# Turning normalised rows by DMA instead of by TensorE in a fused attention and gated-FFN kernel

## The chip, the cores and the metric

The kernel runs on one core of a Trainium2 chip, as one launch. The metric is device time in microseconds (us) of that core. The program has five instruction streams that run side by side and meet at semaphores: TensorE (PE, with its weight loads listed apart as PEld), VectorE (DVE), ScalarE (ACT), GpSimd (POOL) and SyncE (SP), which here only issues DMAs.

## The reference, cut to what matters

One transformer block over 2048 tokens of 512 channels, with 32 heads of 16 channels and a feed-forward width of 1792, all inputs in bf16:

```python
def _layernorm(x, axis=-1, eps=1e-5):
    m = jnp.mean(x, axis=axis, keepdims=True)
    v = jnp.var(x, axis=axis, keepdims=True)
    return (x - m) / jnp.sqrt(v + eps)
...
    def _A_ref(x, wqkv, wo):
        ...
        qkv = (lambda x, *d: x.transpose(*d))((x @ wqkv).reshape(B, S, 3, H, Dh), 2, 0, 3, 1, 4)
        q, k, v = qkv[0], qkv[1], qkv[2]
        scores = jnp.einsum("bhqd,bhkd->bhqk", q, k) * (Dh ** -0.5)
        p = _softmax(scores, axis=-1)
        o = jnp.einsum("bhqk,bhkd->bhqd", p, v)
        return (lambda x, *d: x.transpose(*d))(o, 0, 2, 1, 3).reshape(B, S, D) @ wo

    def _B_ref(x, w_gate, w_up, w_down):
        g = jnp.einsum("bsd,df->bsf", x, w_gate)
        u = jnp.einsum("bsd,df->bsf", x, w_up)
        h = _sigmoid(g) * u
        return jnp.einsum("bsf,fd->bsd", h, w_down)

    x = A_x
    h = x + _A_ref(_layernorm(x, axis=-1), A_wqkv, A_wo)
    h2 = h + _B_ref(_layernorm(h, axis=-1), B_w_gate, B_w_up, B_w_down)
    return h2
```

Both layer norms work on rows (a token on a partition, its 512 channels along the free axis). The projections behind them contract over channels, so the normalised rows have to be turned: channels on partitions, tokens along the free axis. Those turns are what this case is about.

## The kernel before, in words

**Tiling.** Tokens are cut into 16 row tiles of 128, and into four chunks (`c` = 0 to 3) of 512 for the first layer norm. The turned first layer norm of chunk `c` is the tile `xnT[c]`. Attention takes 2048 "units" of 128 keys by 512 queries for a head (or the same area as two key tiles by 256 queries). For each unit PE makes scores into PSUM, ACT (line 1466) or DVE makes them exponentials, and PE multiplies those by the values (line 1260). ACT takes two or three units in one instruction, 128x1024 or 128x1536. DVE takes one unit at a time (line 1284, into a tile `J`), and POOL (line 1305), sometimes with another DVE add (line 1329), derives from `J` further terms of the same exponential. PE then multiplies two or three terms of such a unit instead of one.

**The first layer norm.** Chunk 0 is done in a prologue. For chunks 1 to 3 DVE takes the statistics, POOL makes the reciprocal root and the normalised rows (`pool_apply`, line 589, tile `xn0`), PE turns two row tiles with eight 128x128 transposes (line 732), and DVE copies them from PSUM to `xnT[c]` (line 735). Then PE makes the keys of the first head group (`early_k`, line 745) and the values (`prep_v`, line 318) of that chunk. Attention is already running on the chunks that are there.

**The second layer norm and the FFN.** The FFN runs in eight parts of 256 tokens. For parts 0 to 6 `wo_ln` makes the output projection, adds the residual, normalises on DVE (line 824, tile `hn`), turns each of the two row tiles with four transposes on PE (line 307), and copies them on DVE to half of `xnT[0]` (line 832, read through `hn_of`). `ffn_up` then reads them as the moving operand of the gate and up matmuls (line 841) and `ffn_down` makes the output (line 859). Part 7 comes after the last attention unit, in a tail written out by hand, with turns of its own on PE.

**The order.** The order of every engine is fixed when the program is built. A planner in the kernel keeps a clock for each engine (`T`), charges a cost for each step, and interleaves: for each ACT instruction ("tile n" below) it writes the next scores, then fills PE with value products and with background steps (turns, projections, FFN), each once its inputs are due. It also decides which units go to DVE. The dictionary `PLAN` overrides some of its choices, by tile number and step. What it writes is final: an engine whose next instruction isn't ready waits, whatever stands behind. SP has one queue for the loads of the gate and up weights (`wgu`, line 849), the residual rows (`xr`, line 785), the output stores (line 867) and the rest, in the order in which the planner wrote them.

The planner knows a step that ends later than its job by a fixed time:

```python
    class Later:
        def __init__(self, job, ns):
            self.job, self.ns = job, ns

        @property
        def end(self):
            return None if self.job.end is None else self.job.end + self.ns
```

Of the kernel before, what the change touches and what calls it, by code (L numbers as in the profile page):

```python
# [22 lines left out]
PLAN = {124: 2, 159: 2, 178: 9, 193: 3, 194: 3, 207: 2, 224: 9, 239: 2, 334: 1, 354: 1, 384: 9, 385: 9, 416: 3, 464: 9, 466: 1, 476: 1, 512: 3, 527: 2, 529: 9, 530: 3, 540: 1, 559: 1, 641: 5, 720: 2, 737: 3, 769: 4, 800: 3, 801: 4, 833: 5, 865: 9, 942: 2, 945: 9, 1041: 3, 1056: 3, 1071: 2, 1105: 9, 1169: 9, 1345: 4, 1409: 4, 1519: 2, 1520: 4, 1567: 2, 1580: 1, 1598: 3, 1616: 2, 1618: 9, 1632: 3, 1633: 4, 1808: 4, 1824: 1, 1855: 2, 1857: 1, 1888: 9, 1889: 2, 1921: 4, 1922: 3, 1936: 3, 1952: 5, 1968: 4, 2176: 9, 2208: 5, 2224: 9, 2240: 1, 2258: 5, 2284: 2, 2304: 3, 2336: 9, 2352: 2, 2368: 4, 2400: 9, 2401: 3, 2402: 2, 2416: 3, 2432: 1, 2449: 4, 2588: 2, 2604: 2, 2640: 4, 2658: 4, 2688: 9, 2722: 1, 2736: 4, 2780: 1, 2786: 1, 2799: 2, 2831: 2, 2833: 1, 2865: 1, 2866: 5, 2928: 3, 2959: 2, 2976: 4, 2992: 2, 3025: 3, 3056: 3, 3058: 4, 3072: 1, 3102: 3, 3121: 3, 3152: 3, 3164: 1, 3185: 9, 3198: 3, 3200: 4, 3246: 1, 3248: 4, 3249: 2, 3260: 1, 3280: 4, 3297: 4, 3308: 1, 3505: 9, 3551: 2, 3567: 2, 3596: 1, 3649: 3, 3664: 1, 3680: 4, 3695: 1, 3714: 3, 3777: 3, 3808: 2, 3824: 2, 4017: 2, 4046: 3, 4112: 3, 4113: 2, 4145: 3, 4208: 4, 4220: 1, 4224: 3, 4240: 4, 4241: 1, 4284: 1, 4334: 2, 4384: 1, 4526: 3, 4588: 1, 4593: 4, 4608: 5, 4652: 1, 4671: 2, 4719: 2, 4720: 1, 4764: 1, 4768: 4, 4796: 1, 4815: 2, 4816: 1, 4848: 1, 4892: 1, 4912: 5, 4992: 3, 5008: 3, 5009: 3, 5072: 3, 5089: 4, 5090: 4, 5201: 1, 5233: 1, 5263: 1, 5292: 1, 5343: 2, 5356: 1, 5406: 1, 5422: 3, 5425: 4, 5455: 2, 5521: 1, 5548: 1, 5553: 4, 5617: 4, 5628: 1, 5649: 1, 5713: 3, 5728: 3, 5792: 5, 5809: 2, 5824: 1, 5858: 9, 5890: 9, 5918: 2, 6002: 4, 6017: 4, 6047: 2, 6048: 2, 6064: 2, 6140: 1, 6156: 2, 6160: 2, 6208: 4, 6304: 4, 6321: 1, 6383: 1, 6431: 2, 6433: 4, 6524: 1, 6529: 9, 6544: 4, 6545: 4, 6608: 2, 6673: 1, 6684: 1, 6720: 4, 6796: 2, 6800: 3, 6848: 3, 6865: 1, 6896: 5, 6927: 2, 6956: 1, 6960: 4, 6978: 5, 7106: 2, 7120: 3, 7122: 4, 7164: 1, 7200: 4, 7248: 9, 7406: 1, 7440: 4, 7454: 3, 7490: 9, 7553: 3, 7585: 4, 7598: 3, 7648: 4, 7649: 4, 7660: 1, 7663: 1, 7696: 4, 7712: 4, 7729: 4, 7759: 1, 7760: 3, 7762: 2, 7776: 3, 7777: 1, 7809: 2, 7824: 1, 7826: 9, 7841: 9, 7857: 9, 7873: 9, 7921: 3, 7969: 1, 7985: 4, 8000: 4, 8065: 4, 8076: 1, 8128: 4, 8144: 1, 8156: 2, 8161: 9, 8176: 2, 8192: 1, 8193: 2, 8204: 2, 8240: 2, 8272: 4, 8274: 4, 8287: 1, 8289: 4, 8304: 1, 8332: 2, 8400: 4, 8512: 2, 8578: 9, 8620: 2, 8623: 2, 8652: 2, 8656: 1, 8703: 2, 8766: 1, 8768: 2, 8800: 1, 8844: 1, 8849: 3, 8863: 2, 8879: 2, 8880: 3, 8914: 2, 8926: 1, 8930: 3, 8944: 3, 8976: 4, 8992: 3, 8994: 9, 9008: 1, 9025: 1, 9040: 4, 9042: 5, 9074: 2, 9120: 4, 9152: 1, 9168: 3, 9201: 4, 9232: 3, 9308: 1, 9312: 4, 9346: 1, 9425: 5, 9438: 2, 9488: 1, 9500: 1, 9520: 4, 9521: 3, 9538: 9, 9564: 1, 9569: 9, 9598: 1, 9612: 1, 9726: 2, 9740: 1, 9760: 4, 9777: 4, 9826: 4, 9872: 3, 9888: 3, 9904: 4, 9916: 1, 9969: 3, 9983: 2, 10064: 3, 10108: 2, 10114: 9, 10144: 4, 10176: 3, 10192: 3, 10193: 1, 10239: 2, 10242: 3, 10268: 2, 10272: 2, 10273: 3, 10321: 9, 10384: 2, 10386: 4, 10428: 1, 10498: 1, 10510: 1, 10512: 4, 10513: 1, 10524: 2, 10542: 1, 10544: 2, 10560: 3, 10561: 9, 10591: 2, 10640: 5, 10673: 1, 10753: 3, 10784: 3, 10785: 3, 10849: 1, 10864: 4, 10944: 1}  # L23
# [121 lines left out]
def kernel(  # L145
# [11 lines left out]
    nc = tc.nc  # L157
# [51 lines left out]
    xnT = [const.tile([P, DC, QC], BF16, name=f"xnT{c}") for c in range(NQC)]  # L209
    KT = [const.tile([P, S], BF16, name=f"KT{p}") for p in range(NP)]  # L210
# [100 lines left out]
    def proj8(ps, w_sb, p, c, a=0, b=DC):  # L311
        for d in range(a, b):
            nc.tensor.matmul(ps, lhsT=w_sb[:, d, p * P:(p + 1) * P], rhs=xnT[c][:, d, :],  # L313
                             start=(d == 0), stop=(d == DC - 1))

    def v_mm(ps, t, a=0, b=DC):
        for d in range(a, b):
            nc.tensor.matmul(ps, lhsT=xnT[t // TQ][:, d, (t % TQ) * P:(t % TQ + 1) * P],  # L318
                             rhs=wv_sb[:, d, :], start=(d == 0), stop=(d == DC - 1))
# [73 lines left out]
    def copy0(c, i, eng):  # L393
        eng(out=xnT[c][:, :, i * P:(i + 1) * P], in_=buf["t", c, i])
        free0(("t", i))

    def proj0(which, i):
        ps = buf[which] if which in buf else buf.setdefault(which, bank0(which))
        for d in range(DC):
            E.matmul(ps[:, i * P:(i + 1) * P], lhsT=w0[:, which, d, :], rhs=xnT[0][:, d, i * P:(i + 1) * P],  # L400
                     start=(d == 0), stop=(d == DC - 1))
# [185 lines left out]
    def pool_apply(c, i):  # L587
        xn = buf["xn", c, i] = prep.tile([P, D], BF16, name="xn0", bufs=4)
        nc.gpsimd.tensor_scalar(out=xn[:], in0=xb[c][:, i, :], scalar1=mvs[c][:, i, 0:1],
                                scalar2=rstds[c][:, i:i + 1], op0=ALU.add, op1=ALU.mult)  # L590

    TINY = 400.0
# [62 lines left out]
    DRAIN = 170.0  # L655
    OVER = 300.0
# [50 lines left out]
    def early_ln(c):  # L707
# [14 lines left out]

        done["ap", c] = ja

        def turn():
            for i in range(0, TQ, 2):
                yield pe(4, pm_new, ja[i], ja[i + 1], ns=8 * 75.0)
                ps = pm_tile()
                pt = ps.bitcast(BF16).rearrange("p (i b q) -> p i b q", i=2, b=DC)
                for k in range(2):  # L730
                    for b in range(DC):
                        nc.tensor.transpose(out=pt[:, k, b, :],
                                            in_=buf["xn", c, i + k][:, b * P:(b + 1) * P],
                                            identity=ident_bf[:])
                pm_out(dve(605, lambda i=i, pt=pt: nc.vector.tensor_copy(
                    out=xnT[c][:, :, i * P:(i + 2) * P].rearrange("p b (i q) -> p i b q", i=2),
                    in_=pt), st["mark"]))
                done["x", c, i // 2] = [st["pms"][-1]]
        return turn()

    def early_k(c):
        yield pe(4, pm_new, After(("x", c, 0)), After(("x", c, 1)))
        ps = pm_tile()
        for d in range(DC):
            nc.tensor.matmul(ps, lhsT=w0[:, 0, d, :], rhs=xnT[c][:, d, :],
                             start=(d == 0), stop=(d == DC - 1))
        done["k0", c] = [pm_out(dve(603, lambda: nc.vector.tensor_copy(
            out=KT[0][:, c * QC:(c + 1) * QC], in_=ps), st["mark"]))]
# [39 lines left out]
    def hn_of(r):  # L788
        o = r % 2 * PW
        return xnT[0][:, :, o:o + PARTS[r][2]]  # L790

    def wo_ln(r):
# [27 lines left out]
        hns, jh = {}, {}  # L820

        def apply(i):
            hn = hns[i] = fwork.tile([P, D], BF16, name="hn", bufs=2)
            nc.vector.tensor_scalar(out=hn[:], in0=h[:, i, :], scalar1=mv[:, i, 0:1],
                                    scalar2=rstd[:, i:i + 1], op0=ALU.subtract, op1=ALU.mult)
        for i in range(n):
            jh[i] = dve(455, lambda i=i: apply(i), jr[i])
        jx = []
        for i in range(n):
            yield pe(2, pm_new, jh[i], ns=300.0)  # L830
            pt = transpose4(pm_tile(), hns[i])
            jx.append(pm_out(dve(335, lambda pt=pt, i=i: nc.vector.tensor_copy(
                out=hn_of(r)[:, :, i * P:(i + 1) * P], in_=pt), st["mark"])))
        done["hn", r] = jx
# [4 lines left out]
    def gate_mm(ps, w, r, a=0, b=DC):  # L839
        for d in range(a, b):  # L840
            nc.tensor.matmul(ps[:, 0:PARTS[r][2]], lhsT=w[:, d, :], rhs=hn_of(r)[:, d, :],  # L841
# [153 lines left out]
    def place_now(job):  # L995
# [6 lines left out]
        elif isinstance(job, Job) and job.end is None:  # L1002
            for d in job.deps:
                place_now(d)
            if job.end is None and job.ready() is not None:
# [35 lines left out]
    PART = 12 + 8 * FC // 2 + 14 * (PW // P)  # L1041
# [86 lines left out]
    def finish_group(qc, g):  # L1128
# [13 lines left out]
        def turn():  # L1142
# [13 lines left out]
            if g == NG - 1 and qc < NCH - 1:  # L1156
                rs = [r for r in range(NR) if PARTS[r][0] == qc]
                for k, r in enumerate(rs):
                    queue(wo_ln(r), ("wo", r), 6 * (PARTS[r][2] // P), k)
# [249 lines left out]
    for c in range(1, NQC):  # L1409
        queue(lns[c], ("ln", c), 8)  # L1410
# [210 lines left out]
    for i in range(n):  # L1621
        pt = transpose4(gu[i], hnl[i])
        dst = hn_of(r)[:, :, i * P:(i + 1) * P]
# [76 lines left out]
```

## Time and profile before

| what | value |
|---|---|
| time, median of 3 runs | 742.64 us (742.5 to 743.09) |
| the profiled execution: its time | 743.0 us |
| its span in the trace | 741.1 us |
| PE busy | 707.3 us |
| DVE busy | 672.1 us |
| ACT busy | 708.0 us |
| POOL busy | 418.1 us |
| granted TensorE clock | full in all 40 slices |
| share of DMA queue q1 | 18.3% of 16 engines |

"Busy" is the union of an engine's instructions in the trace. Matmuls overlap and their ends are modelled, so PE's share says little of how near its peak it is. A group's row gives the count, the busy time of the group and the mean duration of one. Where instructions of one engine overlap, busy divided by count is less than the mean. The time is about 1.9 us more than the span of the same execution, which begins and ends with the core's own instructions.

### The profile page before, as it was taken

Reading aid. Unit: us, or ns where it says so; the run is one execution under the profiler, and the core shown is the slowest. Engines: PE = TensorE matmul, PEld = TensorE weight load, DVE = VectorE, ACT = ScalarE, POOL = GpSimd, SP = SyncE. Lnnn points to the kernel's source line nnn. Section 1 sums busy time; section 2 is a strip of 40 time slices with the busy share of each in tenths; the row PEclk is TensorE's granted clock in tenths of the full one; section 3 lists DMA queues with packets and bytes.
Section 4 is the critical chain, followed back from the end, with each engine's and each line's share of the span. In section 5 each row is a group of like instructions: output and inputs, shape, how many; then the busy total and the mean of one; then the engine's idle time right before and its main releaser. Section 6 shows DMA issues by size and latency. Waiting matters only on the chain.

```text
span 741.1 us, 26337 instructions
## 1 busy us (share of the span) xinstructions
PE 707.3 (95%) x11142; PEld 342.0 (46%) x11213; DVE 672.1 (91%) x1334; ACT 708.0 (96%) x789; POOL 418.1 (56%) x711
## 2 busy tenths in 40 slices
PE   8989998888999999999999999999999999999997
PEld 3332223443555445544555455444554455455555
DVE  6988999999999999998999899989999999999952
ACT  7989999999999999999999999999999999999962
POOL 2533466677466557655655556556655666756710
PEclk9999999999999999999999999999999999999999
DMA  7000005000123103310222123201231034003270
GB/s 241 1 1 2 1 1 172 4 2 2 31 79 88 31 10 101 88 31 15 73 59 60 38 65 103 59 9 36 76 88 31 17 101 116 24 10 88 59 214 18
DMA packets 68923, 41.59 MB, mean 56 GB/s; under 512 B 3520, under 2 KB 68800, under 8 KB 68800
## 3 DMA queue, kind: packets, MB, share of 16 engines
q1 hardware_dynamic: 68512, 39.59, 18.3%
q8 instruction: 89, 1.46, 0.8%
q14 instruction: 34, 0.28, 0.1%
q10 hardware_dynamic: 288, 0.26, 0.1%
HBM read 37.75 MB, written 2.10 MB: 54 GB/s over the span
## 4 chain that ended last, share of the span: by engine, by line
PE 56%; ACT 26%; DVE 13%; issue 3%; POOL 1%; ACTq 0%; POOLq 0%; DVEq 0%
ACT pt L1466 19%; PE PS L1102 19%; PE PS L1260 15%; PE PS L841 10%; DVE J L1284 6%; PE PS L859 5%; ACT xnT L1466 3%; PE PS L313 2%; PE PS L318 2%; DVE J L1329 1%; ACT QTb L1466 1%; PE PS L780 1%; ACT th L871 1%; POOL J L1305 1%; PE PS L474 1%
## 5 line engine op out<-in xcount | busy, mean ns | idle before, releaser
L1305 POOL INT64_ADD J<-J x642 | 400.0, 636 | 267.2 <-DVE J L1284 228.3
L1466 ACT ACTIVATE pt<-PS 128x1024 f16<-128x1024 f32 (+2 forms) x517 | 517.4, 1137 | 5.5 <-PE PS L1102 4.8
L1284 DVE TENSOR_SCALAR J<-PS 128x512 int16<-128x512 f32 x613 | 403.0, 677 | 19.6 <-PE PS L1102 15.0
L1102 PE MATMUL PS<-QT,KT 32*128 32x256 bf16 (+1 forms) x3712 | 265.3, 276 | 17.0 <-ACT pt L1466 9.7
L1260 PE MATMUL PS<-J,Vaug 128*17 128x256 f16 (+1 forms) x3128 | 221.0, 279 | 1.6 <-DVE xs L1168 0.6
L1260 PE MATMUL PS<-pt,Vaug 128*17 128x256 f16 (+1 forms) x2048 | 189.8, 278 | 0.5 <-issue 0.5
L1102 PEld LDWEIGHTS <-KT 32*128 32x128 bf16 x3840 | 91.5, 92 | 202.6 <-issue 197.2
L1260 PEld LDWEIGHTS <-Vaug 128*17 128x17 bf16 x5797 | 129.8, 90 | 78.8 <-issue 70.7
L841 PE MATMUL PS<-xnT,wgu 128*128 128x256 bf16 x784 | 113.4, 274 | 0.6 <-DVE qd L768 0.2
L1466 ACT ACTIVATE xnT<-PS 128x1024 f16<-128x1024 f32 (+1 forms) x88 | 96.5, 1140 | 0.1
L1329 DVE TENSOR_TENSOR J<-J 128x1024 f16<-128x1024 f16 (+1 forms) x107 | 77.7, 727 | 9.1 <-POOL J L1305 8.5
L841 PEld LDWEIGHTS <-wgu 128*128 128x128 bf16 x784 | 64.0, 97 | 39.8 <-issue 34.2
L859 PE MATMUL PS<-wd,hT 128*128 128x512 bf16 x173 | 51.6, 383 | 2.2 <-issue 2.1
L1260 PE MATMUL PS<-xnT,Vaug 128*17 128x256 f16 x358 | 53.1, 273 | 0.0
L871 ACT ACTIVATE th<-PS 128x512 f32<-128x512 f32 (+1 forms) x63 | 39.2, 622 | 8.8 <-DVE hT L854 5.6
L1466 ACT ACTIVATE QTb<-PS 128x1024 f16<-128x1024 f32 x39 | 42.9, 1100 | 0.1
L913 DVE SCALAR_TENSOR_TENSOR hT<-th,PS 128x512 bf16<-128x512 f32 x49 | 33.1, 675 | 1.7 <-PE PS L841 1.6
L1168 DVE STREAM_TRANSPOSE xs<-PS 128x256 f32<-128x256 f32 (+1 forms) x60 | 27.3, 455 | 2.3 <-PE PS L1260 2.0
L1466 ACT ACTIVATE xb<-PS 128x1024 f16<-128x1024 f32 (+2 forms) x26 | 26.8, 1098 | 1.4 <-PE PS L1102 0.9
L1466 ACT ACTIVATE pe<-PS 128x1024 f16<-128x1024 f32 (+2 forms) x26 | 25.5, 1027 | 2.5 <-PE PS L1102 1.9
L1260 PE MATMUL PS<-QTb,Vaug 128*17 128x256 f16 x156 | 25.8, 274 | 0.0
L1139 DVE TENSOR_TENSOR o<-xs,rsum 128x128 bf16<-128x128 f32 (+1 forms) x60 | 22.7, 378 | 2.1
(129 smaller groups left out, 416.4 us busy)
## 6 DMA issues: line engine op xcount, KB each, us to landing
wgu<-in_B_w_gate_dram SPq DMA_DIRECT2D x49, 256.0 KB, 3.0
wgu<-in_B_w_up_dram SPq DMA_DIRECT2D x49, 256.0 KB, 3.5
out_dram<-ob SPq DMA_DIRECT2D x16, 128.0 KB, 2.0
wd<-in_B_w_down_dram SPq DMA_DIRECT2D x1, 1792.0 KB, 7.6
xr<-in_A_x_dram SPq DMA_DIRECT2D x14, 128.0 KB, 3.6
xb<-in_A_x_dram SPq DMA_DIRECT2D x6, 256.0 KB, 6.5
J<-in_B_w_gate_dram SPq DMA_DIRECT2D x4, 384.0 KB, 6.0
J<-in_B_w_up_dram SPq DMA_DIRECT2D x4, 384.0 KB, 6.8
```

The lines of the kernel that those rows point to most:

```text
L841: nc.tensor.matmul(ps[:, 0:PARTS[r][2]], lhsT=w[:, d, :], rhs=hn_of(r)[:, d, :], start=(d == 0), stop=(d == DC - 1))
L859: nc.tensor.matmul(ps, lhsT=hT[:, f, i * P:(i + 1) * P], rhs=wd[:, f, :], start=(f == 0), stop=(f == FC - 1))
L871: nc.scalar.activation(out=th[:, 0:ps.shape[-1]], in_=ps, func=ACT.Tanh, scale=0.5)
L913: nc.vector.scalar_tensor_tensor(out=hT[:, f:f + k, 0:w], in0=th[f][:].rearrange("p (k n) -> p k n", k=k), scalar=1.0, in1=ps2.rearrange(" ...
L1102: nc.tensor.matmul(pss[:, ui, i * CW[qc]:(i + 1) * CW[qc]], lhsT=KT[g // 2][32 * j:32 * j + 32, k * P:(k + 1) * P], rhs=q[32 * j:32 * j + ...
L1139: nc.vector.tensor_tensor(out=o2[:, 0:w // 32, DH * a:DH * a + DH], in0=xs[:, 0:w // 32, 0:DH], in1=rec.to_broadcast([P, w // 32, DH]), op ...
L1168: j = dve(650 - ns[0], lambda: nc.vector.transpose(out=xs[:, 0:w // 32, :].rearrange("p b r -> p (b r)"), in_=src), LAST, st["xs"], pr=-1)
L1260: nc.tensor.matmul(dst[32 * j:32 * j + VW, 0:w], lhsT=un.v[:, kt * SPAN[qc] + i, h, :], rhs=un.ap[:, i * w:(i + 1) * w], start=clears and ...
L1284: nc.vector.tensor_scalar(out=J[:, 0, k, :], in0=src, scalar1=ZOFF, scalar2=float(-min(CHORDS)), op0=ALU.add, op1=ALU.max)
L1305: nc.gpsimd.int64_add(words(s), words(0), CHORDS[s - 1] * (1 + 2 ** 16 + 2 ** 32 + 2 ** 48))
L1329: nc.vector.tensor_tensor(out=f1, in0=f1, in1=J[:, 0, 0:k, :].bitcast(FP16), op=ALU.add)
L1466: ex = nc.scalar.activation(out=pt, in_=pss[:, 0:wa, :], func=ACT.Exp, scale=AS)
```

## The change

The turns of the second layer norm for parts 0 to 6 (14 row tiles), and those of chunks 2 and 3 of the first one (8 row tiles), become DMA transposes from SBUF to SBUF on SP's queue, issued where the normalised rows are written. PE's 88 transposes for them and DVE's 18 copies from PSUM are gone. Chunks 0 and 1 and the tail's part 7 stay on PE. The turned tiles are laid out anew, each row tile's four blocks of 128 channels side by side (`xnv`), so that one DMA writes 128x4x128 elements in one piece per partition. Matmuls that read several row tiles now read pieces of 128 columns that lie 512 columns apart. The planner counts the turned rows as due 3000 ns after the normalisation (`DMA_T`), and its `PLAN` is another.

```diff
-PLAN = {124: 2, 159: 2, ...
+PLAN = {176: 5, 239: 2, ...
...
+    xnv = [x[:].rearrange("p d q -> p (d q)").rearrange("p (i d q) -> p i d q", d=DC, q=P) for x in xnT]
...
     def proj8(ps, w_sb, p, c, a=0, b=DC):
         for d in range(a, b):
-            nc.tensor.matmul(ps, lhsT=w_sb[:, d, p * P:(p + 1) * P], rhs=xnT[c][:, d, :],
+            nc.tensor.matmul(ps.rearrange("p (i q) -> p i q", q=P), lhsT=w_sb[:, d, p * P:(p + 1) * P], rhs=xnv[c][:, :, d, :],
                              start=(d == 0), stop=(d == DC - 1))
...
         xn = buf["xn", c, i] = prep.tile([P, D], BF16, name="xn0", bufs=4)
         nc.gpsimd.tensor_scalar(out=xn[:], in0=xb[c][:, i, :], scalar1=mvs[c][:, i, 0:1],
                                 scalar2=rstds[c][:, i:i + 1], op0=ALU.add, op1=ALU.mult)
-
+        if c in TURN_DMA:
+            nc.sync.dma_start_transpose(out=xnv[c][:, i], in_=xn[:])
+
+    TURN_DMA = (2, 3)
...
+    DMA_T = 3000.0
...
+        if c in TURN_DMA:
+            done["ap", c] = [Later(j, DMA_T) for j in ja]
+            for i in range(0, TQ, 2):
+                done["x", c, i // 2] = done["ap", c][i:i + 2]
+            return None
         done["ap", c] = ja
...
     def hn_of(r):
         o = r % 2 * PW
-        return xnT[0][:, :, o:o + PARTS[r][2]]
+        return (xnT[0][:].rearrange("p d q -> p (d q)")[:, DC * o:DC * (o + PARTS[r][2])]
+                .rearrange("p (i d q) -> p i d q", d=DC, q=P))
...
         def apply(i):
-            hn = hns[i] = fwork.tile([P, D], BF16, name="hn", bufs=2)
+            hn = fwork.tile([P, D], BF16, name="hn", bufs=2)
             nc.vector.tensor_scalar(out=hn[:], in0=h[:, i, :], scalar1=mv[:, i, 0:1],
                                     scalar2=rstd[:, i:i + 1], op0=ALU.subtract, op1=ALU.mult)
+            nc.sync.dma_start_transpose(out=hn_of(r)[:, i], in_=hn[:])
         for i in range(n):
             jh[i] = dve(455, lambda i=i: apply(i), jr[i])
-        jx = []
-        for i in range(n):
-            yield pe(2, pm_new, jh[i], ns=300.0)
-            pt = transpose4(pm_tile(), hns[i])
-            jx.append(pm_out(dve(335, lambda pt=pt, i=i: nc.vector.tensor_copy(
-                out=hn_of(r)[:, :, i * P:(i + 1) * P], in_=pt), st["mark"])))
-        done["hn", r] = jx
+        done["hn", r] = [Later(jh[i], DMA_T) for i in range(n)]
...
     def gate_mm(ps, w, r, a=0, b=DC):
         for d in range(a, b):
-            nc.tensor.matmul(ps[:, 0:PARTS[r][2]], lhsT=w[:, d, :], rhs=hn_of(r)[:, d, :],
+            nc.tensor.matmul(ps[:, 0:PARTS[r][2]].rearrange("p (i q) -> p i q", q=P), lhsT=w[:, d, :], rhs=hn_of(r)[:, :, d, :],
                              start=(d == 0), stop=(d == DC - 1))
...
-            if job.end is None and job.ready() is not None:
+            if job in gq:
+                run_pool()
+            elif job.end is None and job.ready() is not None:
...
-    PART = 12 + 8 * FC // 2 + 14 * (PW // P)
+    PART = 8 + 8 * FC // 2 + 14 * (PW // P)
```

## The prediction

> **What bounds the kernel now.** I read the page's busy times first, then a table of windows, since a mean over the span mixes stages.
>
> ```profile
> PE 707.3 (95%) x11142; PEld 342.0 (46%) x11213; DVE 672.1 (91%) x1334; ACT 708.0 (96%) x789; POOL 418.1 (56%) x711
> ```
>
> PE and ACT are both nearly full, DVE almost, so busy shares alone don't name a bound. The windows (columns: length, then busy of PE, PEld, DVE, ACT, POOL) do:
>
> ```profile
> 25.00:50.00 25.00, 21.90 (x146) 8.19 (x149) 21.43 (x43) 21.55 (x24) 11.90 (x23) 1.00 0.01 2
> 50.00:120.00 70.00, 66.51 (x628) 19.27 (x638) 62.80 (x111) 66.63 (x68) 32.33 (x53) 1.00 0.06 18
> 120.00:700.00 580.00, 562.41 (x9890) 283.20 (x9947) 548.69 (x1078) 577.81 (x633) 359.70 (x578) 1.00 0.19 54
> 700.00:741.00 41.00, 35.58 (x349) 22.20 (x343) 20.27 (x49) 20.79 (x37) 5.95 (x10) 1.00 0.36 105
> ```
>
> From 120 to 700 us ACT is idle 2.2 us of 580. The early stage leaves ACT 3.4 us idle between 25 and 50 us. After 700 us comes the tail, which the change doesn't touch. The next question is whether a busy ACT is working or stretched. The timeline of ACT (start, duration) answers:
>
> ```profile
> 51.38 1.45 ACT L1466 ACTIVATE pt<-PS 128x1536 f16<-128x1536 f32 x1
> 52.73 4.26 ACT L1466 ACTIVATE xb<-PS 128x1024 f16<-128x1024 f32 x5
> ...
> 524.85 0.79 ACT L871 ACTIVATE th<-PS 128x512 f32<-128x512 f32 x1
> 525.33 1.23 ACT L1466 ACTIVATE xnT<-PS 128x1024 f16<-128x1024 f32 x1
> 526.23 1.24 ACT L1466 ACTIVATE pt<-PS 128x1024 f16<-128x1024 f32 x1
> ```
>
> Starts count here, not durations, because the next instruction starts before the last ends: 0.48 us after a 512-wide one, 0.90 after a 1024-wide one, 1.35 after a 1536-wide one. So ACT is bound by its own work. What shortens the kernel is ACT work taken away, or an ACT wait in the early stage taken away, as long as PE and DVE keep up. The transposes themselves are in these groups:
>
> ```profile
> L832 DVE COPY xnT<-PS 128x512 bf16<-128x512 bf16 x14 | 5.7, 409 | 0.0
> L307 PE MATMUL PS<-ident_bf,hn 128*128 128x128 bf16 x56 | 5.5, 221 | 0.2
> L735 DVE COPY xnT<-PS 128x1024 bf16<-128x1024 bf16 x6 | 4.0, 676 | 0.2 <-PE PS L732 0.2
> L732 PE MATMUL PS<-ident_bf,xn 128*128 128x128 bf16 x48 | 3.5, 220 | 0.2 <-issue 0.2
> ```
>
> Neither group made anybody wait. They cost room on PE and DVE, not latency.
>
> **The change part by part.** The planner writes another order, so I compare the instruction lists of the two built programs and price the differences by rows (busy over count; ACT by spacing).
>
> PE: 56 transposes of `hn` (5.5) and 32 of the 48 of `xn` (3.5 x 32/48 = 2.3) go: -7.8 us. Five dummy matmuls (L673, 4.5/12 = 0.38) go: -1.9. New are 64 value products of 256 columns (199.4/2982 = 0.067) and 10 of 512 (21.6/146 = 0.15): +5.8. Sum about -4 us.
>
> DVE: 14 copies (-5.7) and 4 of the 6 of chunks 1 to 3 (-2.7) go. Twelve 1024-wide adds (L1329, 72.3/95 = 0.76) go and two 512-wide ones come: -8.2. Two more instructions at L1311 go: -1.3. Ten more units come to DVE (L1284, 403.0/613 = 0.66): +6.6. Sum about -11 us.
>
> ACT: it had 639 exponentials of 1024, 50 of 1536 and 7 of 512; it gets 651, 40 and 3. The ten units that DVE gains, ACT loses. By spacing: 12 x 0.90 - 10 x 1.35 - 4 x 0.48 = -4.6 us. This is the term on the path that sets the end, spread over the span, at full value wherever ACT has no gap.
>
> POOL: 16 more adds (400.0/642 = 0.62): +10 us, covered by its 267 us of idle before that line. If that cover went, DVE's adds at L1329 would wait (8.5 us in all now).
>
> SP: 22 more issues, at about the 0.4 to 0.5 us that the issue of a weight load takes in SP's timeline. SP mostly stands and waits for a weight buffer to be released by PE:
>
> ```profile
> SPq L849 <- PE PS L1102: 374.1, 47, 72.6
> ```
>
> Behind a transpose that waits for `hn` stand weight loads, residual rows and stores. DVE's `hn` comes within a tile or two of where the list has it, and two weight buffers alternate some 5 to 11 us apart in SP's timeline, so I cost this at nothing; if that cover is gone, the gate matmuls (L841) are late. Chunks 2 and 3: their eight transposes stand behind the first loads, whose issues end at 10 us, and ahead of `wd`, which waits until 105 us; also nothing.
>
> The early stage: the keys of chunk 3 (L745) stand in tile 28 instead of 34, since the statistics, POOL's rows and the turns follow each other without the ring of PSUM tiles. In ACT's timeline the gaps from 40 to 47 us, where the old order brings chunk 3's turn and keys, add up to 0.81 + 0.21 + 0.33 + 0.48 + 0.50 = 2.3 us. I take 1.0 of it: some of the gaps stem from DVE's value copies, which stay.
>
> The pieces of 128 columns in the moving operand: no row shows one. Below, nothing (a gain has no ground, the columns are the same). Above, as if each piece were a matmul of its own: 2 x 0.098 (L307) against 113.4/784 = 0.145 at L841, 0.05 x 784 = 40 us of PE. I take nothing: the rows follow the columns (272 ns for 256 at L1102, 273 at L841) and the instruction count stays.
>
> **How long a DMA transpose takes** is the disputed cost. No row shows one. The nearest are transfers of the same 128 KB:
>
> ```profile
> out_dram<-ob SPq DMA_DIRECT2D x16, 128.0 KB, 2.0
> xr<-in_A_x_dram SPq DMA_DIRECT2D x14, 128.0 KB, 3.6
> ```
>
> By these it lands 2.0 to 3.6 us after issue, and several overlap (1792 KB of `wd` in 7.6 us is 0.5 us for 128 KB). The Trainium skill speaks against the change: "VectorE: DVE Perf Modes", section "The three transpose paths", gives 1309 ns for one 128x128 bf16 block by DMA and 390 ns by TensorE, and its rules keep such a turn on TensorE where PSUM will do. The row says 220 ns for TensorE's block, 98 ns of busy, so the page is too high there. By the page one DMA of four blocks would be 5.2 us, estimated. "DMA: Bandwidth & Descriptors", section "Latency and other measured facts", gives 261 GB/s for a DMA transpose: estimated 0.5 us for 128 KB. The two fit together only if most of the 1309 ns is paid once per DMA. I take 3 us and overlap, as in the rows, and keep 2.0 and 5.2 one at a time as ends.
>
> Who waits? In the list the first gate matmul of a part stands 5, 7, 27, 37, 17, 18 and 5 tiles behind its second transpose. At 1.07 us a tile (741.1/694), parts 0 and 6 leave 5.3 us. 3 us is hidden, 5.2 alone is too. In the early stage POOL's third pair of row tiles takes 24.06 to 27.03 us; four such pairs put the eighth transpose near 35.9, and the keys of chunk 3 would start near 39.4 (tile 28 was at 38.5 us, and those keys come some 0.9 later): slack 3.5 us. Hidden at 3, tight at 3.6.
>
> **Sum** against the profiled execution: 743.0 (span 741.1 and 1.9 around it) - 4.6 - 1.0 = 737.4. The median shown is 0.4 below the profiled execution, so 737.0 as a median.
>
> **Rivals.** (1) *The transposes queue up, slower.* If they are served one at a time, the first starts near 26.3 us and the eighth lands at 26.3 + 8s. Keys of chunk 3, on PE in order, hold up the scores and so ACT. With s = 3.0 us that is 50.3 against 39.4: 10.9 us late; part 0 loses 2 x 3.0 - 5.3 = 0.7. 742.6 - 5.6 + 11.6 = 748.6. With the page's 5.2 us it is 28.5 + 5.1 late, 770. It decides from s = (39.4 + 5.6 - 26.3)/8 = 2.3 us. For it: the page, and that nothing here shows a transpose. Against: transfers of this size overlap in the trace. Chance 0.27, and 0.03 for the pieces of 128 columns. (2) *No change*: ACT loses its 4.6 us of work but waits as much more, since PE's room of 4 us is small and ten more units bring POOL and value work; or the transposes are 5 us late once. 742.6, chance 0.08. (3) *Faster still*: all 2.3 us of the gaps go and half of ACT's other early idle (1.7 of the 3.4 between 50 and 120 us): 742.6 - 4.6 - 2.3 - 1.7 = 734.0, part of the faster 0.62. That the change doesn't do what it says is excluded by the lists: 88 transposes gone, 22 DMAs in.
>
> **How the numbers follow.** Measurement can tell about 0.2%, 1.5 us. Faster: forecast 0.50 and rival 3 with 0.12. Same 0.08, slower 0.30. The likeliest case alone spans 734 to 740. The range goes from 733.5, below rival 3, to 750, past rival 1 at s = 3.0, leaving out its upper part (some 0.1) and little below.
>
> **What would show it.** Right: ACT busy near 703, idle from 120 to 700 us still under 5 us, copies at L832 gone, transposes landing in 2 to 4 us, PE's keys of chunk 3 near 40 us with no wait for a DMA. Wrong: PE waiting at the gate matmuls or early keys for `xnT<-hn` or `xnT<-xn`, ACT idle between 25 and 60 us above 5 us, or weight loads late behind a waiting transpose; or a longer mean at the gate matmul's row.

## The result and the profile after

| | before | after |
|---|---|---|
| median of 4 runs each, same chip | 742.57 us (742.3 to 743.09) | 735.09 us (734.57 to 735.42) |
| the profiled execution: time, span | 743.0, 741.1 us | 735.08, 733.3 us |

The ratio is 0.9898, with a 95% interval of 0.9881 to 0.9915: 7.5 us less, where 5.6 were forecast. The page's busy times after (engine, busy, share of the span, instructions):

```profile
PE 712.8 (97%) x11194; PEld 337.8 (46%) x11194; DVE 663.3 (90%) x1314; ACT 703.1 (96%) x787; POOL 421.8 (58%) x727
```

ACT is down from 708.0 to 703.1, DVE from 672.1 to 663.3, POOL up by 3.7. PE seems up by 5.5, but this can't be compared: before shows 11142 matmuls beside 11213 weight loads, so records are missing there, and after shows as many of the one as of the other.

The windows after (length, then busy of PE, PEld, DVE, ACT, POOL, the clock, DMA share, GB/s):

```profile
25.00:50.00 25.00, 23.87 (x137) 6.72 (x136) 21.06 (x44) 22.44 (x25) 11.45 (x21) 1.00 0.22 43
50.00:120.00 70.00, 69.30 (x757) 20.83 (x754) 66.94 (x116) 69.44 (x75) 42.15 (x71) 1.00 0.07 22
120.00:700.00 580.00, 570.89 (x9962) 283.37 (x9959) 543.70 (x1065) 577.29 (x634) 359.26 (x584) 1.00 0.21 59
700.00:733.00 33.00, 28.03 (x210) 17.99 (x203) 12.62 (x34) 12.81 (x28) 0.33 (x1) 0.99 0.34 103
```

The second row is the one to read. From 50 to 120 us ACT was idle 3.4 us and is now idle 0.56; POOL does 42.15 us of work there against 32.33, DVE 66.94 against 62.80. Between 25 and 50 us ACT's idle time goes from 3.45 to 2.56 only. From 120 to 700 us it is 2.2 before and 2.7 after.

The new DMAs: the issues (count, median us from issue to landing), the records of the `hn` transposes (duration on SP's queue min/median/max in ns, then their waiters and landings), and SP's timeline for the `xn` ones:

```profile
xnT<-hn SPq DMA_TRANSPOSE x14, 2.4
xnT<-xn SPq DMA_TRANSPOSE x8, 2.4
```

```profile
L837 SPq DMA_TRANSPOSE xnT<-hn x14: 1189/1198/2057, 182.7 to 649.7; - x14
...
PE PS L847: 0.2, 1
...
DMA to landing us min/median/max: 2.4/2.4/4.0
```

```profile
25.61 11.91 SPq L593 DMA_TRANSPOSE xnT<-xn  x8
```

A transpose of 128 KB lands 2.4 us after its issue begins, and the issue holds SP's queue for 1.2 us. In all of the kernel PE waited once for one of the 14, 0.2 us, and never for one of the 8. The gate matmuls, which now read two pieces of 128 columns, take what they took (a mean of 275 ns against 274, a median of 273 in both):

```profile
L841 PE MATMUL PS<-xnT,wgu 128*128 128x256 bf16 x784 | 113.4, 274 | 0.6 <-DVE qd L768 0.2
```

```profile
L847 PE MATMUL PS<-xnT,wgu 128*128 128x256 bf16 x784 | 112.4, 275 | 0.7 <-DMA xnT<-hn 0.2 <-DVE qd L778 0.2 <-DVE hT L919 0.2
```

**Where the time came from.** A list of busy times doesn't show when a lead arises. Attention is 2048 units in both kernels, so the traces can be laid side by side by progress: the start of the ACT or DVE exponential that completes the k-th unit (L1466 and L1284 before, L1475 and L1292 after). "Lead" is how much sooner the changed kernel gets there. The time from one ACT start to the next is the work (0.90 us after a 1024-wide one, and so on, as in the prediction); what is over that is stall.

| units | lead of after at the end of the stretch, us | ACT's work, before to after | stall, before to after |
|---|---|---|---|
| 0 to 60 | -0.7 (late) | 25.0 to 25.4 | 3.5 to 3.8 |
| 60 to 125 | 3.0 | 23.4 to 22.5 | 3.3 to 0.4 |
| 125 to 250 | 5.8 | 40.1 to 38.4 | 2.2 to 1.1 |
| 250 to 400 (158.6 us before, 151.2 after) | 7.4 | 45.6 to 45.2 | 2.3 to 1.1 |
| 400 to 2048 | 8.9 | 536.0 to 533.8 | 12.9 to 13.5 |

7.4 us of the lead are there at 151 us, before the first row of the second layer norm is turned (182.7 us). Of the sums, 4.8 us are ACT work that went to DVE and 4.2 us are stalls. The two come one after the other: at unit 125 DVE has taken 16 units in both kernels, so the 3.0 us of lead there are mostly stalls; at unit 250 it has taken 58 against 53, at the end 623 against 613. The tail gives 1.1 us back: the last exponential is 1536 wide instead of 1024, and ACT then waits 1.55 us against 1.17 for PE.

The largest waits of ACT between 45 and 150 us, before and then after (who, for whom: sum, times, longest):

```profile
ACT pt L1466 <- PE PS L1102: 2.4, 3, 1.5
ACT xb L1466 <- PE PS L1102: 0.9, 3, 0.5
...
```

```profile
ACT xb L1475 <- PE PS L1110: 0.3, 1, 0.3
ACT pt L1475 <- PE PS L1110: 0.2, 1, 0.2
```

The early chain itself, before and then after: POOL's last normalised rows and its first adds for DVE's units, and the keys of chunk 3 on PE:

```profile
39.76 1.53 POOL L589 TENSOR_SCALAR xn<-xb,mv,rstd 128x512 bf16<-128x512 bf16 x2
47.25 1.99 POOL L1305 INT64_ADD J<-J  x4 [5.96 <-DVE KT L747]
...
45.18 1.03 PE L745 MATMUL PS<-xnT,w 128*128 128x512 bf16 x4
```

```profile
34.23 1.55 POOL L590 TENSOR_SCALAR xn<-xb,mv,rstd 128x512 bf16<-128x512 bf16 x2
41.62 1.94 POOL L1313 INT64_ADD J<-J  x4 [5.83 <-DVE Vaug L324]
...
40.17 1.03 PE L755 MATMUL PS<-xnT,w 128*128 128x512 bf16 x4
```

The rows are written 5.5 us sooner, the adds begin 5.6 us sooner and the keys 5.0. It is tempting to see the cause of the lead in this. Two things speak against it. DVE takes units before POOL's first add, three of them after and seven before, so it doesn't depend on POOL for that. And the pair of kernels without overrides, below, has the same lead at unit 125 with POOL's adds no sooner. (POOL stands idle for some 6 us ahead of its first add in all twelve traces, 5.8 to 6.1 us. The planner books 9 us once at this place; what it is, no run here shows.)

### The profile page after: what moved, and what is told of

Its sections match the earlier page's. It is cut to its first block, busy times and chain, and to the rows that moved or that the text cites. A ratio compares the mean times of both kernels' runs of the same rounds, so it can differ in the third digit from the quotient of the medians.

```text
span 733.3 us, 26424 instructions
## 1 busy us (share of the span) xinstructions
PE 712.8 (97%) x11194; PEld 337.8 (46%) x11194; DVE 663.3 (90%) x1314; ACT 703.1 (96%) x787; POOL 421.8 (58%) x727
## 3 DMA queue, kind: packets, MB, share of 16 engines
q1 hardware_dynamic: 80480, 42.48, 20.5%
## 4 chain that ended last, share of the span: by engine, by line
PE 55%; ACT 22%; DVE 17%; issue 3%; POOL 2%; DMA 0%; POOLq 0%; DVEq 0%; ACTq 0%
PE PS L1110 18%; PE PS L1268 15%; ACT pt L1475 15%; PE PS L847 9%; DVE J L1292 8%; PE PS L865 6%; ACT xnT L1475 2%; DVE J L1337 2%; POOL J L1313 2%; PE PS L314 2%; PE PS L319 2%; PE PS L790 1%; ACT th L877 1%; DVE st L274 1%; ACT xb L1475 1%
## 5 line engine op out<-in xcount | busy, mean ns | idle before, releaser
L1475 ACT ACTIVATE pt<-PS 128x1024 f16<-128x1024 f32 (+1 forms) x512 | 513.3, 1128 | 3.9 <-PE PS L1110 2.8
L1292 DVE TENSOR_SCALAR J<-PS 128x512 int16<-128x512 f32 x623 | 410.8, 678 | 22.3 <-PE PS L1110 16.5
L1268 PE MATMUL PS<-J,Vaug 128*17 128x256 f16 (+1 forms) x3218 | 226.8, 279 | 0.9 <-DVE xs L1176 0.3
L1268 PE MATMUL PS<-pt,Vaug 128*17 128x256 f16 (+1 forms) x2021 | 191.9, 279 | 0.0
L1268 PEld LDWEIGHTS <-Vaug 128*17 128x17 bf16 x5871 | 132.2, 90 | 79.7 <-issue 74.5
L1475 ACT ACTIVATE xnT<-PS 128x1024 f16<-128x1024 f32 (+1 forms) x88 | 96.3, 1131 | 0.0
L847 PEld LDWEIGHTS <-wgu 128*128 128x128 bf16 x784 | 64.5, 98 | 38.7 <-issue 33.0
L1337 DVE TENSOR_TENSOR J<-J 128x1024 f16<-128x1024 f16 (+1 forms) x97 | 67.8, 701 | 9.7 <-POOL J L1313 9.3
L865 PE MATMUL PS<-wd,hT 128*128 128x512 bf16 x196 | 56.7, 384 | 0.0
L1475 ACT ACTIVATE QTb<-PS 128x1024 f16<-128x1024 f32 x39 | 43.2, 1108 | 0.3 <-PE PS L1110 0.3
L1475 ACT ACTIVATE xb<-PS 128x1024 f16<-128x1024 f32 (+2 forms) x29 | 29.9, 1093 | 0.3 <-PE PS L1110 0.3
L1475 ACT ACTIVATE pe<-PS 128x1024 f16<-128x1024 f32 (+2 forms) x26 | 26.0, 1061 | 1.7 <-PE PS L1110 1.6
L1147 DVE TENSOR_TENSOR o<-xs,rsum 128x128 bf16<-128x128 f32 (+1 forms) x60 | 24.2, 403 | 2.1
```

The costliest lines, as they stand in the source:

```text
L847: nc.tensor.matmul(ps[:, 0:PARTS[r][2]].rearrange("p (i q) -> p i q", q=P), lhsT=w[:, d, :], rhs=hn_of(r)[:, :, d, :], start=(d == 0), sto ...
L865: nc.tensor.matmul(ps, lhsT=hT[:, f, i * P:(i + 1) * P], rhs=wd[:, f, :], start=(f == 0), stop=(f == FC - 1))
L1147: nc.vector.tensor_tensor(out=o2[:, 0:w // 32, DH * a:DH * a + DH], in0=xs[:, 0:w // 32, 0:DH], in1=rec.to_broadcast([P, w // 32, DH]), op ...
L1268: nc.tensor.matmul(dst[32 * j:32 * j + VW, 0:w], lhsT=un.v[:, kt * SPAN[qc] + i, h, :], rhs=un.ap[:, i * w:(i + 1) * w], start=clears and ...
L1292: nc.vector.tensor_scalar(out=J[:, 0, k, :], in0=src, scalar1=ZOFF, scalar2=float(-min(CHORDS)), op0=ALU.add, op1=ALU.max)
L1337: nc.vector.tensor_tensor(out=f1, in0=f1, in1=J[:, 0, 0:k, :].bitcast(FP16), op=ALU.add)
```

## The experiments

Three explanations of the gain stand side by side. Theory W: it is ACT's work, some 4.6 us that the freed DVE and PE time lets the planner move to DVE, wherever a turn is taken off TensorE. Theory E: it is the early stage alone, its chain freed of TensorE and PSUM. The third: the overrides of `PLAN`, which differ, happen to be better.

### The two turns one at a time

An override is bound to a tile number, so a kernel with half of the change can't use the whole dictionary of either. Four kernels therefore keep only the early part, up to tile 174. The two with chunks 2 and 3 on TensorE keep that of the kernel before, the two with these chunks by DMA that of the changed one. So a step between the two pairs changes the early overrides too. For the changed one's:

```diff
-PLAN = {176: 5, 239: 2, ... 10912: 1, 10913: 1}
+PLAN = {176: 5, 239: 2, ... 2767: 1}
```

With only the second layer norm by DMA, also:

```diff
-    TURN_DMA = (2, 3)
+    TURN_DMA = ()
```

and with only chunks 2 and 3, `hn` is turned on PE again, into the new layout (and the planner's counts of steps, `PART` and that of `wo_ln`, are again those of before):

```diff
-            nc.sync.dma_start_transpose(out=hn_of(r)[:, i], in_=hn[:])
...
-        done["hn", r] = [Later(jh[i], DMA_T) for i in range(n)]
+        jx = []
+        for i in range(n):
+            yield pe(2, pm_new, jh[i], ns=300.0)
+            pt = transpose4(pm_tile(), hns[i])
+            jx.append(pm_out(dve(335, lambda pt=pt, i=i: nc.vector.tensor_copy(
+                out=hn_of(r)[:, i], in_=pt), st["mark"])))
+        done["hn", r] = jx
...
```

Neither turn by DMA:

> The kernel before, with its table of planner overrides kept only up to tile 174 and empty from tile 175 on (just ahead of the first turn of the second layer norm). It is the base of a 2 x 2 comparison: neither turn by DMA. By the instruction list ACT's exponentials are 652.2 us of spacing, 4.6 more than before. Theory W (time follows ACT's work, wherever it is): 742.6 + 4.6 = about 747. Theory E (the gain arises in the early stage, up to about 150 us, from chunks 2 and 3): it says nothing of this kernel alone; also 745 to 750.

The second layer norm only:

> Second layer norm turned by DMA, chunks 2 and 3 on TensorE; overrides of the kernel before up to tile 174, none after. ACT's exponentials are 647.6 us. Theory W: about 742.5, 4.6 below the base. Theory E: the early stage is the base's, so the turns of the second layer norm, whose PE and DVE work lies beside a busy ACT, bring little: within 1.5 us of the base.

Chunks 2 and 3 only:

> Chunks 2 and 3 turned by DMA, second layer norm on TensorE; overrides of the changed kernel up to tile 174, none after. ACT's exponentials are 648.3 us. Theory W: 4 us below the base by ACT's work, and 1 us of early gaps. Theory E: 6 to 8 us below the base, and nearly as good as both.

Both:

> Both by DMA; overrides of the changed kernel up to tile 174, none after. ACT's exponentials are 642.3 us. Theory W: 10 us below the base, about 737, and 6 below the kernel with chunks 2 and 3 alone. Theory E: 6 to 8 below the base, within 1.5 us of the kernel with chunks 2 and 3 alone.

| by DMA | median, us | ratio to before, interval | ACT's exponential work, counted by spacing | lead over "neither" at unit 400 |
|---|---|---|---|---|
| neither | 756.02 | 1.0181 (1.0164 to 1.0198) | 652.2 | |
| second layer norm | 751.25 | 1.0112 (1.0095 to 1.0129) | 647.6 | 0.0 |
| chunks 2 and 3 | 751.99 | 1.0120 (1.0103 to 1.0137) | 648.3 | 4.0 |
| both | 748.04 | 1.0069 (1.0052 to 1.0086) | 642.3 | 7.1 |

The second layer norm brings 4.8 us, the chunks (with their early overrides) 4.0, both 8.0: nearly a sum. ACT's work falls by 4.6, 3.9 and 9.9. So W comes near the size for each half, and E fails for the second layer norm, of which it expected nearly nothing, and for the chunks, of which it expected nearly all.

Three reservations go with this. First, W holds for steps, not for levels: "neither" was expected near 747 and took 756.02, and the kernel with the second layer norm alone divides its units between ACT and DVE just as the kernel before does (639 exponentials of 1024, 50 of 1536, 7 of 512, and 613 on DVE) and is 8.7 us slower. So most of what the overrides save is stall, and ACT's work alone doesn't give a time. Second, single stalls of some us lie in these kernels. The profile of "both" has one near 390 us, where ACT waits 5.8 us for PE and PE 2.8 us for DVE, and its granted clock is 0.5 for 3.4 us; "neither" has 10.2 us at a clock of 0.5, each half 3.4 (the last 6 us left out), and the full kernels before and after have none behind the first 7 us. So the sizes are good to a few us, and that they nearly add up is partly chance. Third, where the time comes differs. The chunks' 4.0 us are there at unit 400 and stay about that until unit 800. The second layer norm alone leads by nothing before unit 1000 or so. In company it also helps early: 7.1 us at unit 400 against 4.0, although nothing of it has run by then. Chunks alone and both divide their units alike up to unit 152 (75 us); after that the planner has fewer background steps to place and places them otherwise. By unit 250 DVE has taken 53 units with neither, 53 with the second layer norm, 54 with the chunks and 58 with both, while POOL's adds begin at the same time in the last two (41.5 and 41.7 us).

### No overrides at all

Does the early lead come from the overrides? Two more kernels, before and after the change, with an empty dictionary:

```diff
-PLAN = {...}
+PLAN = {}
```

> The kernel before with an empty dictionary of overrides, to be read against its pair, the changed kernel with an empty one. Both theories: slower than before, since half of the overrides gone cost 13 us; 755 to 765. By the counts of the program ACT has 647.1 us of exponential work here.

> The changed kernel with an empty dictionary of overrides. Its early order owes nothing to overrides. By the counts ACT has 641.5 us of exponential work, 5.6 less than the pair. Theory 'the change gives room on ACT, and its early chain is shorter': 6 to 12 us below the pair, with a lead of 3 to 7 us already by the 400th unit. Theory 'the early lead comes from the overrides found for the new order': the lead by the 400th unit is under 1.5 us, and the difference at the end 4 to 6 us, ACT's work alone.

They took 754.53 us (754.22 to 754.74) and 747.55 us (747.37 to 747.71): 7.0 us less by the change, 7.5 with the dictionaries. At unit 400 the lead is 4.3 us, made of 1.8 us less ACT work and 2.7 us less stall by the same counting (4.5 from the first unit on, which itself starts 0.1 us later). So the change brings its gain without any override, and most of it early. Where the dictionaries differ, the lead at unit 400 is 7.4 rather than 4.3; those 3 us can't be credited to the turns alone. The third theory explains a part of where the gain lies, and little of its size.

The pair also shows what the early chain has to do with it. The same instructions as above, before and then after, without overrides:

```profile
33.70 1.87 POOL L589 TENSOR_SCALAR xn<-xb,mv,rstd 128x512 bf16<-128x512 bf16 x2
41.48 1.98 POOL L1305 INT64_ADD J<-J  x4 [5.91 <-issue]
...
41.17 1.04 PE L745 MATMUL PS<-xnT,w 128*128 128x512 bf16 x4
```

```profile
33.97 1.78 POOL L590 TENSOR_SCALAR xn<-xb,mv,rstd 128x512 bf16<-128x512 bf16 x2
41.86 5.69 POOL L1313 INT64_ADD J<-J  x10 [6.10 <-DVE Vaug L324]
...
40.17 1.03 PE L755 MATMUL PS<-xnT,w 128*128 128x512 bf16 x4
```

POOL's rows and adds come no sooner by the change (41.86 us against 41.48), and the keys of chunk 3 by 1.0 us, not 5.0. The late chain of the kernel before belongs to its overrides. Yet the lead at unit 125 is 2.7 us here, 2.9 in the step from neither to the chunks, and 3.0 with the full dictionaries. So the gain up to there goes with turning the chunks by DMA, and not with POOL being free or the keys being ready some 5 us sooner. Which of the freed pieces of PE and DVE time makes it was not tested.

### The layout alone

The kernel before, order and dictionary unchanged, every turn on PE, only the tiles laid out as in the change and read in pieces of 128 columns (the diff is that of `xnv`, `proj8`, `v_mm` and `gate_mm` in the change):

> The kernel before with its own overrides and its own order, all turns on TensorE; only the layout of the turned tiles is the new one, so that the moving operands of the gate, up, key and query matmuls come in pieces of 128 columns. Prediction: nothing, within 0.2% of 742.6, and 273 ns at the gate matmul's row. Rival (each piece as a matmul of its own): up to 40 us more.

742.99 us (10 runs) against 742.65; the ratio is 1.0001 (0.9992 to 1.0011). The group of its gate matmul:

```profile
L852 PE MATMUL PS<-xnT,wgu 128*128 128x256 bf16 x784 | 113.5, 274 | 0.6 <-DVE qd L778 0.2
```

The same mean of 274 ns with two pieces as with one. Of the 40 us that the prediction kept as an upper end nothing shows.

### Transposes doubled and tripled to the same place

These ask how much room the transposes have: each of the 8, issued twice; then each of the 14, three times.

```diff
         if c in TURN_DMA:
             nc.sync.dma_start_transpose(out=xnv[c][:, i], in_=xn[:])
+            nc.sync.dma_start_transpose(out=xnv[c][:, i], in_=xn[:])
```

> The changed kernel with each of the eight transposes of chunks 2 and 3 issued twice, same source and same place, in the same order of all other instructions. At 1.2 us of issue each, the sixteen take from 25.6 to about 45 us, so the last turn of chunk 3 lands near 46 instead of 39. If early lateness is paid in full (rival 1 of the prediction as a mechanism, theory E): 3 to 7 us slower, 738 to 742. If ACT catches up later because only its work counts (theory W in its pure form): under 1 us.

```diff
             nc.sync.dma_start_transpose(out=hn_of(r)[:, i], in_=hn[:])
+            nc.sync.dma_start_transpose(out=hn_of(r)[:, i], in_=hn[:])
+            nc.sync.dma_start_transpose(out=hn_of(r)[:, i], in_=hn[:])
```

> The changed kernel with each of the 14 transposes of the second layer norm issued three times, nothing else changed. Six issues of 1.2 us put the landing 8.4 us behind the first issue instead of 3.6. The gate matmuls stand 5.3 us behind in parts 0 and 6, and 7 us and more in the others: 2 to 3 us late twice, 737 to 741, if the wait on PE is paid in full; parts 1 to 5 hide it. If the queue of weight loads behind them is what hurts, it is more, and all parts pay: 745 and up. If neither: 735.

753.74 us and 765.82 us, both far over what was expected, with ratios of 1.0143 (1.0126 to 1.0159) and 1.0314 (1.0291 to 1.0336). SP's timeline of the first and its waits in the second show why:

```profile
25.30 1.32 SPq L593 DMA_TRANSPOSE xnT<-xn  x1
27.84 1.19 SPq L594 DMA_TRANSPOSE xnT<-xn  x1
29.12 1.22 SPq L593 DMA_TRANSPOSE xnT<-xn  x1
31.55 1.19 SPq L594 DMA_TRANSPOSE xnT<-xn  x1
...
51.44 1.26 SPq L593 DMA_TRANSPOSE xnT<-xn  x1
53.92 1.19 SPq L594 DMA_TRANSPOSE xnT<-xn  x1
```

```profile
SPq L838 <- DMA xnT<-hn: 24.3, 14, 4.3
SPq L839 <- DMA xnT<-hn: 19.7, 14, 2.9
```

The repeat writes where the first is still writing, so SP waits for it to land: 2.5 us, then 1.2 for the next. A pair costs SP 3.7 us instead of 2.5, and the last of the eight lands near 56.3 us instead of 38.7. What that does to PE and ACT, in the waits and in ACT's timeline:

```profile
PE PS L756 <- DMA xnT<-xn: 14.8, 2, 8.8
```

```profile
43.99 0.60 ACT L1476 ACTIVATE pe<-PS 128x512 f16<-128x512 f32 x1 [6.99 <-PE PS L1111]
...
58.97 1.94 ACT L1476 ACTIVATE pt<-PS 128x1024 f16<-128x1024 f32 x2 [10.62 <-PE PS L1111]
```

The kernel is 18.6 us above the changed one and already 19.0 us behind at unit 100: lateness at the early keys is paid in full and never made up. PE's longest waits in the tripled one:

```profile
PE PS L849 <- DMA xnT<-hn: 21.1, 3, 9.5
...
PE PS L849 <- DMA wgu<-in_B_w_gate_dram: 4.4, 1, 4.4
```

The first three fall at parts 0, 1 and 6, which have the fewest tiles between the rows and the gate matmul (5, 7 and 5 by the prediction). The fourth, at 420 us, is a weight load late behind the repeats on SP: the cover that the prediction named for SP's queue, gone. By progress the four cost 11.5, 7.3, 5.5 and 7 us in order of time (parts 0 and 1, the late load, part 6): 31 us, against 25.5 of waiting. The rest fits what the clock does. Around each of these waits the granted clock is 0.5 for a while, here for the first and the last (length, busy of PE, PEld, DVE, ACT, POOL, the clock, DMA share, GB/s):

```profile
191.36:201.60 10.24, 5.00 (x51) 2.07 (x52) 1.98 (x3) 2.58 (x3) 0.97 (x2) 0.50 0.13 27
...
679.47:686.29 6.82, 3.62 (x34) 1.59 (x38) 1.08 (x2) 1.96 (x3) 1.11 (x2) 0.50 0.10 21
```

The two waits of the doubled kernel have such stretches too, 6.8 and 10.2 us long; the changed kernel has no such wait, and none between 6 and 732 us. Neither of the two kernels measures the room cleanly, since SP's own waits and the clock come on top. They do show rival 1 at work: transposes that land late hold up PE, and with it ACT, for good.

### Transposes added to another place

The same question again, without the wait. Each of chunk 2's four rows is first turned into chunk 3's tile, which is still empty, each into its own part:

```diff
         if c in TURN_DMA:
+            if c == 2:
+                nc.sync.dma_start_transpose(out=xnv[3][:, i], in_=xn[:])
             nc.sync.dma_start_transpose(out=xnv[c][:, i], in_=xn[:])
```

> The changed kernel, with each of the four row tiles of chunk 2 also turned into the still empty tile of chunk 3 ahead of its own transpose: four more transposes, none of which writes where another in flight writes. Theory 'SP's issue of about 1.25 us sets the pace, the flights overlap, and the slack at the keys of chunk 3 is 1.5 us': issues from 25.6 every 1.25 us, chunk 2 landed at 36.8 (keys of it wanted at 35.9), the last transpose landed at 41.8 against 38.7, keys of chunk 3 some 1.6 us late, and the kernel 1.6 us longer than the changed one: 736 to 737.5. Theory 'transposes are served one at a time, 2.5 us each, wherever they write': pairs take 3.7 us as in the earlier doubled run, the last lands at 47, keys 7 us late, 741 to 744.

737.94 us (737.64 to 738.65), ratio 0.9932 (0.9915 to 0.9948), 2.85 us above the changed kernel (2.6 if each is set against the runs of before on its own chip). SP's timeline, the landings of the tile's transposes, and the early keys in PE's timeline:

```profile
25.47 1.32 SPq L594 DMA_TRANSPOSE xnT<-xn  x1
26.84 1.25 SPq L595 DMA_TRANSPOSE xnT<-xn  x1
28.19 1.21 SPq L594 DMA_TRANSPOSE xnT<-xn  x1
29.44 1.26 SPq L595 DMA_TRANSPOSE xnT<-xn  x1
...
34.67 6.51 SPq L595 DMA_TRANSPOSE xnT<-xn  x5
```

```profile
DMA to landing us min/median/max: 2.4/2.5/2.6
```

```profile
37.31 1.02 PE L757 MATMUL PS<-xnT,w 128*128 128x512 bf16 x4 [1.52 <-DMA xnT<-xn]
42.60 1.02 PE L757 MATMUL PS<-xnT,w 128*128 128x512 bf16 x4 [0.83 <-DVE Vaug L323]
```

The issues follow each other at 1.25 to 1.4 us, although each takes 2.4 to 2.6 us to land. So transposes do overlap in flight; what they take one at a time is SP's issue. The overlap theory is confirmed, and serving one at a time (741 to 744) is out. The size is over its 736 to 737.5. Chunk 2's last row lands at 37.2 us, as worked out (36.8), and the keys of chunk 2 start at 37.31 instead of 35.86. But POOL then waits, up to 1.8 us, for a row buffer whose transpose has not landed, and the start of the keys of chunk 3 moves by 2.43 us (42.60 against 40.17). The lead lost at unit 60 is 2.35 us, and it stays. The estimate had no term for the row buffers.

## Why the prediction was right, and where not

- **ACT's work, -4.6 us: right.** By spacing it fell 4.8 us. Its two halves, measured apart, brought 4.8 and 4.0 us. The failed part of the step is "spread over the span, at full value": 3.0 of the 4.8 us fall between units 60 and 400, that is before 151 us.
- **The early stage, -1.0 us: the term that was mis-sized.** By unit 400 stalls are 4.8 us fewer (5.2 fewer after unit 60, 0.3 more before). It was also half misplaced. The gaps from 40 to 47 us, of which 1.0 was taken, went from 2.0 to 0.6 us of idle ACT, but those from 25 to 40 us grew from 1.45 to 1.95, and the greater part of what went lay behind, between 50 and 150 us. Rival 3 had half of ACT's 3.4 us between 50 and 120 us go; 2.8 did. The mechanism given for this term doesn't hold as it stands. The keys of chunk 3 do start sooner, at 40.17 us instead of 45.18, but the reason given, turns without the ring of PSUM tiles, brings 1.0 us in the pair without overrides; the rest came with the order of the overrides. That pair shows 2.7 us fewer stalls by unit 400, so some 2 of the 4.8 us depend on that order as well. What in it does it wasn't tested.
- **The tail, which the change "doesn't touch": it gave back 1.1 us**, by how the last exponentials fell into widths, and the stalls after unit 400 grew by 0.6. So the gain was larger than forecast because the early term was 3.8 us too small, against these 1.7 that were not deducted. That 735.1 lies as near to 737.0 as it does is partly luck: two errors of opposite sign.
- **How long a transpose takes, 3 us and overlapping: right in kind.** It is 2.4 us to landing. The issue on SP was taken at 0.4 to 0.5 us from weight loads and is 1.2. This sets the pace: 1.25 us from one to the next where rows are ready, under the 2.3 us from which rival 1 decides. By the Trainium skill's price for a block (1309 ns, in "VectorE: DVE Perf Modes", section "The three transpose paths") the prediction had estimated 5.2 us for one DMA of four blocks; it measured 2.4. By the rate of 261 GB/s (in "DMA: Bandwidth & Descriptors", section "Latency and other measured facts") it had estimated 0.5 us from one to the next; on this queue it measured 1.25. Neither estimate is near. How the time grows with the number of blocks no run here shows, since all transposes have four.
- **The early slack, 3.5 us: right, and a little small.** Rows came when worked out (the last issue at 36.31 us, against 35.9), and the keys start at 40.17, against 39.4: 3.9 us for the landing, which took 2.4, so 1.5 us were left. At the keys of chunk 2 it is 3.5 (landed at 32.4, read at 35.86). The kernel stands that near to losing: four more transposes cost 2.85 us.
- **The second layer norm hidden: right, but not behind 5.3 us.** Tiles times their mean length put 5.3 us between the second transpose and the first gate matmul of parts 0 and 6. The traces have 2.9 us at part 0 (184.00 to 186.88) and 3.3 at part 6 (649.68 to 653.00). PE waited 0.2 us in all, because the landing took 2.4 us at part 0 and 3.3 at part 6; at the 5.2 us that the prediction called hidden too, it would by the same sum have waited some 2 us at each. What stood behind SP's waiting transposes cost nothing that the trace shows either; SP's waits have one long one at a transpose, and the weight loads still wait mostly for PE to release their buffers:

```profile
SPq L855 <- PE PS L1110: 288.9, 44, 14.7
...
SPq L837 <- DVE J L1337: 60.2, 1, 60.2
```

- **DVE -11 us: -8.8 of busy. POOL +10 us: +3.7**, although its adds went from 642 to 658 as counted, because their mean fell from 636 to 626 ns. It was covered as said: DVE's wait for POOL went from 8.5 to 9.3 us. PE's -4 us can't be seen for the missing records.
- **The pieces of 128 columns: nothing, as taken.**
- **Two readings were slightly off.** "Neither group made anybody wait": DVE waited 0.2 us for the transposes at L732, and PE 0.4 us for a copy at L735. And the gate matmul's row has a mean of 274 ns; 273 is its median.

## What to carry to other kernels

Where ACT, DVE and PE are all nearly full, as here, a job moved to an idle queue was worth what the fullest engine could hand over to the freed ones plus the stalls that went with it, and the place to look for both is a table of progress, not the busy shares. A DMA transpose pays if its reader stands behind it by its landing time (2.4 us here) plus one issue time (1.25 us) for each transpose queued ahead; count both, and count whether two of them write to one place. Read the distance to the reader from a trace where you can: tiles times a mean length gave 5.3 us where 2.9 were to be had. And where an order has been tuned, compare the two kernels without the tuning before you believe a cause seen in the timelines: here the early start of POOL's adds and most of that of the keys belonged to the overrides, while most of the gain did not.

## What the runs showed of the hardware

An SBUF-to-SBUF transpose of 128x512 bf16 holds SP for 1.2 us, where the issue of a 256 KB weight load takes about 0.4 to 0.5, and lands in 2.4 us. It moves small packets; the DMA rows of the page after say:

```profile
DMA packets 80893, 44.49 MB, mean 61 GB/s; under 512 B 15489, under 2 KB 80769, under 8 KB 80769
...
q1 hardware_dynamic: 80480, 42.48, 20.5%
```

Before there were 3520 packets under 512 B, so each of the 22 transposes has 544 of them, and q1's share went from 18.3 to 20.5%. Two transposes to the same place are 2.5 us apart, because SP waits for the first to land before the second; to different places they are 1.25 to 1.4 us apart. A moving operand in two pieces of 128 columns costs TensorE nothing measurable (a mean of 274 ns for 256 columns either way). Around PE's six waits of 4.4 to 9.5 us in the doubled and the tripled kernel the granted clock was 0.5 for 3.4 to 10.2 us.
